# Reordering the end of a one-core attention and spectral-mixing kernel: two pairs' sums set into the last modes, their transposes set ahead of the seventh chunk

## The chip, the cores and the metric

One core of a Trainium2 chip. The metric is device microseconds of one execution, the median of several. "The clock" below is the granted clock of TensorE, 1.00 at full speed.

## The reference, cut to what matters

Causal attention gives x, of 8 batches x 576 positions x 512 channels. Then:

```
X = rfft(x, axis=1)[:, :64]                       # 64 modes
Y = X (complex) times w_r + i w_i, mode by mode   # 64 matrices of 512 x 512, twice
y = irfft(Y, n=576)
u = x + y
out = u + max(u @ w_ch, 0)
```

The kernel streams the 64 + 64 weight matrices from HBM all through the attention. `u @ w_ch` is computed as `x @ w_ch + G (Y @ w_ch)`, where G is the inverse transform as a matrix, so that only the part with Y has to wait for the weights.

## The kernel before: the parts that matter

The modes come in 8 chunks for each of 4 groups of input channels. `modes(g, c)` runs one chunk: sixteen matmuls of 32 columns out of four weight tiles (two of w_r, two of w_i, in the order in which they are loaded). In the last group each chunk is finished: `y_sb` (the sum, by VectorE), `yt` (transposed on TensorE, copied by ScalarE to `yt_sb`), `v` (y @ w_ch, four matmuls, cast by VectorE). Both the rows of y and those of v are spread by DMA into `yv`, from where the inverse transform reads them.

```python
def modes(g, c):
    ps = auxpool.tile([P, DM], FP32, name="yp", tag="aux")
    for x in range(4):                       # four weight tiles
        ...
        for cg in range(4):
            nc.tensor.matmul(ps[32 * cg : 32 * cg + 32, :], ..., wt[(g, c, ri, par)][:, cg, :],
                             start=(x == 0), stop=(x == 3), tile_position=(0, 32 * cg), ...)
    ...                                      # last group: y_sb = ps + y_acc, then
    spread(c, 0, yb)                         # DMA of the rows of y into yv

def x_transposed(i):                         # a pair = two blocks of 128 positions
    for x, (b, T) in enumerate(pairs[i]):
        ps = upool.tile([P, DT, P], FP32, name="xt_ps", tag="u")     # two buffers
        ...                                  # 4 transposing matmuls
        nc.vector.tensor_copy(out=xts[i][:, x], in_=ps)
```

The end of the kernel, after the sixth chunk (c = 5) is done:

```python
c = NCK - 2                                  # the seventh chunk
yb = modes(NG - 1, c)
x_transposed(0)
yt = y_transposed(yb)
x_transposed(1)
y_times_wch(c, yt)                           # v, and its spread into yv
for i in range(NPRE):                        # NPRE = 2 pairs
    x_times_wch(i, False)                    # z = x @ w_ch, 8 matmuls each

start_u(0)                                   # u = x of pair 0
add_y(us[0], 0, 0, slice(0, GK))             # u += G y, chunks 0 to 6
for i in range(NPRE):
    add_y(z_of(i), i, 1, slice(0, GK))       # z += G (y @ w_ch), chunks 0 to 6
yb = modes(NG - 1, NCK - 1)                  # the last modes
...                                          # yt, v, then the last chunk's share of u and z
```

The softmax here doesn't subtract the row's maximum and nothing guards it: scores larger than these inputs give would overflow.

## Time and profile before

| | |
|---|---|
| time, median of 6 (first 3 known at the prediction) | 462.47 us (462.04 to 462.76) |
| TensorE, VectorE, ScalarE, GpSimd busy | 74%, 51%, 48%, 40% |
| chain that ended last | DMA 66%, TensorE 20% |
| last wait for weights on that chain ends | 398.31 us of a span of 460.6 |

How to read it: no engine is full, and the DMA row of the page is full through slice 36 of 40. The kernel waits for weights until 398 us, and the last 62 us are a chain of TensorE work. The change lies between 411 and 423 us. The lines of that stretch are in the prediction.

### The profile page before, as it was taken

What the parts mean: (1) busy time and instruction counts of PE and PEld (TensorE: products, weight loads), DVE (VectorE), ACT (ScalarE), POOL (GpSimd) and SP (SyncE); (2) the same over time, 40 slices, a digit from 0 to 9 for tenths busy, and PEclk for the clock granted to TensorE, in tenths of its full rate; (3) what the DMA queues carried; (4) which work ended last, traced back from release to release, by engine and by line L of the source; (5) the groups of instructions that cost most, each with busy time, mean ns of one, the idle gap of its engine ahead of it and who ended that gap; (6) DMA issues with size and microseconds to landing.
All of it is one profiled execution on the core that took longest, in us unless ns stands there. A gap on an engine that the chain in (4) does not pass through costs nothing.

```text
span 460.6 us, 10231 instructions
## 1 busy us (share of the span) xinstructions
PE 342.9 (74%) x4153; PEld 216.4 (47%) x4185; DVE 233.5 (51%) x523; ACT 219.2 (48%) x382; POOL 182.8 (40%) x269
## 2 busy tenths in 40 slices
PE   1779877966663969947397676888977766589995
PEld 1456655644442646624265444565643432244442
DVE  6775665653332646623254435467544432162675
ACT  1585876554342737734255434466710202040895
POOL 6755545534445455344454443455232232100000
PEclk9997999997777979968778979799987789599999
DMA  9999999999999999999999999999999999993697
GB/s 175 201 203 203 202 201 203 203 204 204 204 204 200 203 199 203 204 205 204 202 200 205 204 204 204 204 202 203 206 210 214 214 214 214 214 210 81 228 309 297
DMA packets 110063, 95.16 MB, mean 207 GB/s; under 512 B 28544, under 2 KB 105216, under 8 KB 110016
## 3 DMA queue, kind: packets, MB, share of 16 engines
q0 software_dynamic: 98960, 81.81, 112.1%
q1 hardware_dynamic: 11056, 12.70, 8.9%
q8 instruction: 33, 0.54, 0.4%
q14 instruction: 14, 0.11, 0.1%
HBM read 164.66 MB, written 9.44 MB: 378 GB/s over the span
## 4 chain that ended last, share of the span: by engine, by line
DMA 66%; PE 20%; DVE 6%; issue 4%; POOL 2%; SPq 0%; DVEq 0%; POOLq 0%
DMA w_sb<-in_moe_w_i_dram 29%; DMA w_sb<-in_moe_w_r_dram 20%; DMA q<-in_q_dram 15%; PE z_ps L595 3%; PE sc_ps L365 2%; PE z_ps L654 2%; PE tr_ps L324 2%; PE yp L438 2%; PE u_ps L673 2%; PE u_ps L654 2%; PE sc_ps L359 2%; PE z_ps L774 1%; PE av_ps L394 1%; POOL w_sb L217 1%; DMA xs<-c_negm 1%
## 5 line engine op out<-in xcount | busy, mean ns | idle before, releaser
L373 ACT ACTIVATE p_sb<-sc_ps,cumt_sb 128x576 f16<-128x576 f32 (+1 forms) x256 | 142.0, 635 | 47.1 <-PE sc_ps L365 46.7
L217 POOL DMA_DIRECT2D w_sb<-in_moe_w_i_dram x60 | 45.0, 750 | 79.9 <-PE yp L438 33.5
L217 POOL DMA_DIRECT2D w_sb<-in_moe_w_r_dram x60 | 45.3, 756 | 69.0 <-DMA w_sb<-in_moe_w_r_dram 30.9
L217 POOL DMA_DIRECT2D v<-in_v_dram x72 | 50.7, 707 | 32.4 <-DMA w_sb<-in_moe_w_r_dram 7.8
L438 PE MATMUL yp<-w_sb,xs 128*32 128x512 bf16 x480 | 38.1, 414 | 26.1 <-DMA w_sb<-in_moe_w_i_dram 21.2
L359 PE MATMUL sc_ps<-negm,ident 128*128 128x256 bf16 x256 | 56.3, 306 | 0.2
L324 PE MATMUL tr_ps<-ident,q 64*64 64x64 bf16 x576 | 17.7, 212 | 51.7 <-DMA q<-in_q_dram 51.7
L327 DVE COPY qtA<-tr_ps 64x576 bf16<-64x576 bf16 x32 | 23.7, 742 | 47.4 <-PE tr_ps L324 47.4
L394 PE MATMUL av_ps<-v,p_sb 128*128 128x65 f16 x1024 | 45.0, 199 | 0.0
L344 ACT ACTIVATE p<-sc_ps,cumt 128x64 f16<-128x64 f32 x32 | 10.0, 313 | 73.2 <-PE sc_ps L340 73.2
L394 PEld LDWEIGHTS <-p_sb 128*128 128x128 f16 x1024 | 40.1, 101 | 5.1 <-issue 1.2
L327 DVE COPY ktA<-tr_ps 64x576 bf16<-64x576 bf16 x32 | 24.0, 749 | 32.8 <-PE tr_ps L324 32.8
L438 PEld LDWEIGHTS <-xs 128*32 128x32 bf16 x512 | 22.6, 170 | 37.5 <-issue 34.0
L324 PEld LDWEIGHTS <-q 64*64 64x64 bf16 x576 | 13.8, 124 | 54.4 <-DMA q<-in_q_dram 53.3
L365 PE MATMUL sc_ps<-qtB,ktB 128*128 128x64 bf16 (+2 forms) x160 | 35.2, 326 | 3.7 <-issue 2.4
L365 PE MATMUL sc_ps<-qtA,ktA 65*128 65x512 bf16 (+2 forms) x192 | 37.3, 304 | 0.3 <-DVE ktA L327 0.3
L399 DVE TENSOR_REDUCE den<-av_ps 128x5 f32<-128x10 f32 x64 | 10.8, 169 | 48.6 <-PE av_ps L394 48.6
L404 DVE TENSOR_TENSOR x_all<-av_ps,rcp 128x320 f16<-128x320 f32 x64 | 31.4, 491 | 2.2
L327 ACT COPY ktB<-tr_ps 64x576 bf16<-64x576 bf16 x32 | 20.3, 634 | 20.3 <-DVE ktA L327 19.2
L365 PEld LDWEIGHTS <-ktB 128*128 128x128 bf16 x192 | 22.7, 118 | 15.2 <-issue 6.6
L595 PE MATMUL z_ps<-wch_sb,xs 128*128 128x512 f16 x96 | 28.4, 452 | 0.0
L324 PE MATMUL tr_ps<-ident,k 64*64 64x64 bf16 x576 | 17.4, 209 | 14.5 <-DVE qtB L327 10.7
(103 smaller groups left out, 517.2 us busy)
## 6 DMA issues: line engine op xcount, KB each, us to landing
w_sb<-in_moe_w_r_dram POOLq DMA_DIRECT2D x60, 512.0 KB, 11.9
w_sb<-in_moe_w_i_dram POOLq DMA_DIRECT2D x60, 512.0 KB, 11.9
q<-in_q_dram POOLq DMA_DIRECT2D x32, 144.0 KB, 9.7
k<-in_k_dram POOLq DMA_DIRECT2D x32, 144.0 KB, 10.0
v<-in_v_dram POOLq DMA_DIRECT2D x72, 64.0 KB, 9.8
out_dram<-r_sb SPq DMA_DIRECT2D x16, 256.0 KB, 2.4
out_dram<-r_w SPq DMA_DIRECT2D x16, 256.0 KB, 2.5
x_all<-in_moe_w_i_dram POOLq DMA_DIRECT2D x3, 512.0 KB, 9.8
```

Of the source, the lines that this page charges most:

```text
L217: nc.gpsimd.dma_start(out=dst, in_=src)
L324: nc.tensor.transpose(ps[rows, r, :], src[rows, r, :], ident16[rows, rows])
L327: copy(out=dst[n % NQ][rows, :].rearrange("d (p r) -> d p r", r=R), in_=ps[rows].rearrange("d r p -> d p r"),)
L359: nc.tensor.matmul(ps[:, bass.ds(w * S, W)], ident16, negm[:, bass.ts(r, W)], start=True, stop=False, skip_group_check=True,)
L365: nc.tensor.matmul(ps[:, c0 : c0 + i1 - i0], keys[:, w, r, :], qt[:, i0:i1], start=False, stop=True, skip_group_check=True,)
L373: nc.scalar.activation(out=pt[:, poff[x] : poff[x] + S - w * W], in_=ps[:, w * S : (w + 1) * S - w * W], func=ACTF.Exp, bias=cumt_sb[:, x, ...
L394: nc.tensor.matmul(ps[:, I, r : r + NCH], lhsT, rhs, start=(i == 0), stop=(i == len(todo) - 1), skip_group_check=True,)
L399: nc.vector.tensor_reduce(out=den, in_=ps[:, :, 0 : VW : NCH], axis=mybir.AxisListType.X, op=ALU.add)
L404: nc.vector.tensor_tensor(out=x_all[:, g, b, :, D * h : D * h + D], in0=ps[:, :, 1 : NCH], in1=rcp.unsqueeze(2).to_broadcast([P, NT, D]), ...
L438: nc.tensor.matmul(ps[32 * cg : 32 * cg + 32, :], cols[:, c0 : c0 + 32, c * MC + 2 * cg + par], wt[(g, c, ri, par)][:, cg, :], start=(x == ...
L595: nc.tensor.matmul(z[:, x, :], xts[i][:, x, dt, :], wch_sb[:, dt, :], start=(dt == 0), stop=(last and dt == DT - 1), skip_group_check=True,)
L654: nc.tensor.matmul(dst[x][r, :], G_sb[rows, bass.ds(T * P, r.stop - r.start)], yv[rows, bb, which, :], start=start, stop=True, skip_group_ ...
```

## The change

Intent: give TensorE something to do while it waits for the last weight tile of the last modes (the z sums of two pairs), and while it waits for the seventh chunk's tiles (the transposes of x of these pairs). No instruction is added or removed.

```diff
-    def modes(g, c):
+    def modes(g, c, meanwhile=None):
...
+            if x == 3 and meanwhile:
+                meanwhile()
             for cg in range(4):
...
     c = NCK - 2
+    for i in range(NPRE):
+        x_transposed(i)
     yb = modes(NG - 1, c)
-    x_transposed(0)
     yt = y_transposed(yb)
-    x_transposed(1)
     y_times_wch(c, yt)
...
-    for i in range(NPRE):
-        add_y(z_of(i), i, 1, slice(0, GK))
-    yb = modes(NG - 1, NCK - 1)
+    def first_sums():
+        for i in range(NPRE):
+            add_y(z_of(i), i, 1, slice(0, GK))
+    yb = modes(NG - 1, NCK - 1, first_sums)
```

## The prediction

> **What bounds the kernel now.** I read the page first. Its engine rows show no engine above 74% busy, but its DMA row stands at 9 or more through slice 36 of 40: for most of the span the weight stream is the bound, and the chain that ended last is 66% DMA. The change touches only the last 10%, so I cut the chain of waits to that part.
>
> ```profile
> 398.31 0.04 issue
> 398.36 0.67 PE yp L438 x3
> ...
> 411.47 1.08 PE yp L438 x15
> 412.55 0.02 issue
> 412.57 0.04 DVE y_sb L452
> ...
> 413.18 1.29 DVE xs L589 x2
> 414.47 0.04 issue
> 414.51 0.38 PE xt_ps L585 x4
> 414.89 0.86 PE v_ps L621 x4
> 415.75 3.45 PE z_ps L595 x16
> 419.21 0.43 PE u_ps L673 x2
> 419.64 0.54 PE u_ps L654 x2
> 420.18 0.34 issue
> 420.52 1.02 PE z_ps L654 x4
> 421.54 1.09 PE yp L438 x12
> 422.63 0.02 issue
> 422.65 0.44 DVE y_sb L452
> ```
>
> The columns are start, duration and what held the chain. The last weight wait on the chain ends at 398.31 us. From there to 455 us it is a chain of TensorE work and of copies TensorE waits for. The seventh chunk's modes (411.47) and the last modes (421.54) both start because TensorE got to them, not because a tile arrived. The DMA view gives the w_i tiles a landing of about 21 us after issue. The last one was issued at 398.85 us, so it was there at about 420.2 us, 1.3 us before the last modes began. The seventh chunk's last tile, issued at 387.4 us, was there at about 408.9 us, 2.5 us before its modes. **So the wait that this change is built to fill is hardly there.**
>
> The TensorE timeline of the stretch has all the waits there are:
>
> ```profile
> 412.45 0.62 PE L585 MATMUL xt_ps<-ident16h,x_all 128*128 128x128 f16 x8
> 413.32 0.40 PE L613 MATMUL yt_ps<-ident16h,y_sb 128*128 128x128 f16 x4 [0.25 <-DVE y_sb L452]
> 413.91 0.38 PE L585 MATMUL xt_ps<-ident16h,x_all 128*128 128x128 f16 x4 [0.20 <-DVE xs L589]
> 414.51 0.38 PE L585 MATMUL xt_ps<-ident16h,x_all 128*128 128x128 f16 x4 [0.21 <-DVE xs L589]
> ```
>
> Idle time stands in the brackets: 0.25, 0.20 and 0.21 us, then the 0.34 us ahead of the z sums, which is the arrival of the seventh chunk's y@w_ch rows (issued at 416.51 us, 3.9 us to landing, so 420.4 us). In all 1.0 us in eleven. The transposes of x are what fills the waits of the chain y_sb, yt, yt_sb, v here.
>
> **What the Trainium skill says.** "TensorE: Matmul & The Clock Gate", Part 3, The mechanism: matmuls start and end in program order, only weight loads are pulled ahead. The trace agrees as far as it goes: the z sums wait 0.34 us and the last modes, whose data are there, stay behind them. The same page, Back-to-back issue gap, gives 518 cycles for 512 columns at 2.4 GHz; here 16 matmuls take 3.45 us, 0.216 us each. The same page, Part 1, What's actually happening: half clock after an idle window of about 3.4 us on a free-running grid. The trace agrees on the grid and says how idle: reading windows of 3.41 us aligned on the clock drop at 389.25 us, 1.65 us of TensorE work (338.05 us) was followed by half clock and 1.96 us (382.42 us) was not. "DMA: Bandwidth & Descriptors", Issuing engines are not separate DMA queues: transfers from all issuing engines share the 16 DMA engines and interleave. The trace agrees: a 128 KB spread into yv takes 6.2 us beside the weight stream and 2.9 us after it.
>
> **The change part by part.** No instruction is added or removed; the order listing shows 32 transposing matmuls (counting their loads) moved and 4 z-sum matmuls moved on TensorE, and the seventh y_sb add placed behind the four casts of transposed x on VectorE. I walk the stretch with the durations above, from 411.40 us, where TensorE is free of the last kept product in both kernels.
>
> Transposes ahead of the seventh modes. The first eight take 8 x 0.055 = 0.44 us, from 411.40. VectorE is on the cast of the sixth chunk's v rows until 411.78, so its casts of 0.62 us start at about 411.82. The u buffers are two: the third group of transposes needs the first cast, the fourth the second. In the kernel before, those groups started 0.73 and 1.33 us after the first cast began; so they start at 412.55 and 413.15 here. The first wait (from 412.0, with the drain) is about 0.55 us, the second 0.22. The seventh modes then start at 413.37 instead of 411.40: +1.97 us, of which 0.88 is the transposes themselves.
>
> The seventh chunk's chain without filling. Modes to y_sb: 1.17 us (411.40 to 412.57 before), so y_sb at 414.54; the casts are done by 414.3, so VectorE is free. From y_sb to the first v matmul an unfilled chain took 1.88 us in the chunk at 387.41 to 389.29 us (add 0.69, transposes 0.40, copy 0.58 and three hand-overs). So v at 416.42 us instead of 414.73: **+1.69 us**. TensorE idles some 0.75 us ahead of yt and 0.7 us ahead of v, which the transposes filled before. TensorE's idle time up to v is about 2.2 us against 0.66 us; the 1.5 us agrees with the +1.69, the rest being drains counted as busy.
>
> The products after it do not wait: v 0.86, z 3.45, u 0.43 and 0.43 us, so u is done at 421.6 against 419.9 by the same sum.
>
> The sums between the third and the last weight tile. Twelve mode matmuls at 0.065 us take 0.79 us, to 422.4. The v rows are issued at about 418.2 (v start + 1.8 us, as before); with a landing of 2.9 to 3.9 us that is 421.1 to 422.1, just ahead. So the 0.34 us wait and its 0.1 us of restart are gone, and the last tile, there since about 420.2, is not waited for in either order. Sums 0.9 us, last four modes and drain 0.38 us: the last y_sb at about 423.7 us against 422.65.
>
> Sum: +1.69 from the transposes, -0.6 from the sums' new place (the wait removed, hand-overs), **+1.1 us**. From y_sb on the chain is unchanged and TensorE is 100% busy to 450 us, so nothing absorbs it: 462.7 + 1.1 = **463.8 us**.
>
> **The rivals.**
> 1. The clock drops. In the window 413.14 to 416.55 us my walk leaves TensorE about 0.4 (last transposes) + 1.0 to 1.2 (modes) + 0.4 (yt) + 0.1 (v) = 1.9 us busy, against 2.82 before. That is on the edge between 1.65 (dropped) and 1.96 (did not). A drop at 416.55 would run the v and z matmuls at half rate for one window, 3.41 us, costing about 1.7 us: 465.5. For it: the margin is nothing, and the grid may lie otherwise in other executions. Against: the smallest sliding window I find holds 1.8 us[...]. I give it one in six.
> 2. The change wins. If the last tile came later than I read, or the seventh chunk's, the transposes would cost nothing and the sums would fill a real wait. For it: the DMA row still carries traffic to 419.5 us, so the last tile is the last thing to arrive. Against: both modes started with no weight wait, with 1.3 and 2.5 us in hand. The sums' part alone is worth at most some 0.5 us: 462.2. One in eight for a time under the one of before.
> 3. It is hidden. Later seventh rows find an emptier DMA, so the yv landings move less than the issues, and the walk's idle times shrink if VectorE starts its casts earlier. That gives 463.0. The end has no slack of its own, so full hiding is unlikely.
>
> **Range and chances.** Centre 463.8; below it rival 3 and part of 2, above it the clock. Range 462.4 to 465.9 us. Two per cent is 9.3 us, which no rival reaches: even a clock drop with a late landing stays under 467. Within 2%: 0.98; 0.01 on each side.
>
> **What would show it.** Right: in the changed kernel the seventh modes start near 413.4 us with waits on the casts ahead of them; yt and v of that chunk wait 0.7 us each on y_sb and the copy; the first three weight tiles' twelve matmuls stand ahead of the z sums with no wait; the last y_sb add starts near 423.7 us; from there on both traces are the same. Wrong: a weight-tile wait in either place, a granted clock of 0.5 after 416 us, or a z sum that waits for the v rows. What would make it wrong: a weight stream that ends later in this execution, or transposes that find VectorE free.

## The result and the profile after

463.69 us (463.29 to 464.18, 6 runs) against 462.47 us. A ratio here is the mean time of one kernel's runs over that of the other's of the same rounds, so not quite the ratio of the medians; it is 1.0028, with a 95% interval of 1.0015 to 1.0041. Executions over 1.5% slower than the fastest of the same kernel are left out of the means. The kernel got slower by 1.2 to 1.3 us; at the 2% line it is the same.

The chain of waits of the changed kernel, in the stretch that the prediction shows of the kernel before (start us, duration us, what held the chain):

```profile
413.21 0.38 PE xt_ps L588 x4
413.59 1.08 PE yp L441 x13
...
414.70 0.70 DVE y_sb L455
...
415.45 0.41 PE yt_ps L616 x4
...
415.94 0.59 ACT yt_sb L618
...
416.58 1.04 PE v_ps L624 x4
417.61 3.45 PE z_ps L598 x16
421.07 0.43 PE u_ps L676 x2
421.50 0.51 PE u_ps L657 x2
422.01 0.84 PE yp L441 x10
422.85 0.97 PE z_ps L657 x4
423.81 0.43 PE yp L441 x4
...
424.26 0.44 DVE y_sb L455
```

The y_sb add, the yt transposes, the yt_sb copy and v follow each other here one by one. Before, the first three did not stand on the chain (y_sb for 0.04 us only), because transposes of x ran beside them. The z sums now stand inside the last modes without any wait, where before there was an "issue" of 0.34 us ahead of them. The last y_sb add starts at 424.26 us against 422.65.

TensorE's own timeline has its waits in brackets (idle time, and what ended it):

```profile
412.61 0.38 PE L588 MATMUL xt_ps<-ident16h,x_all 128*128 128x128 f16 x4 [0.56 <-DVE xs L592]
413.21 0.38 PE L588 MATMUL xt_ps<-ident16h,x_all 128*128 128x128 f16 x4 [0.21 <-DVE xs L592]
415.45 0.40 PE L616 MATMUL yt_ps<-ident16h,y_sb 128*128 128x128 f16 x4 [0.80 <-DVE y_sb L455]
416.58 1.04 PE L624 MATMUL v_ps<-wch_sb,yt_sb 128*128 128x512 f16 x4 [0.73 <-ACT yt_sb L618]
421.40 0.61 PE L657 MATMUL u_ps<-yv,G_sb 112*128 112x512 f16 x2
```

These are 2.30 us of idle up to v, against 0.66 us before. The last line has no bracket, but it stands 0.07 us later than two matmuls of 0.216 us behind the start of u would put it: the seventh chunk's rows of y, issued at 415.42 us and 5.9 us on their way, landed at 421.3 us. The kernel before was already as close (0.09 us late by the same sum, its rows issued at 413.29 us and 6.2 us on their way). That will matter.

The clock stayed up. The view by windows, in the windows of 3.41 us aligned on this trace's rise of the clock at 402.22 us (window, its length, busy time of each engine with its instructions, granted clock, DMA share, GB/s):

```profile
412.46:415.87 3.41, 2.22 (x28) 1.33 (x27) 2.58 (x5) 0.20 (x1) 0.00 (x0) 1.00 1.18 204
415.87:419.29 3.42, 2.71 (x13) 1.29 (x14) 0.69 (x1) 0.58 (x1) 0.00 (x0) 1.00 0.58 122
```

The emptiest window kept 2.22 us of TensorE work and the next ran at clock 1.00, so nothing of the loss is clock. The grid lay kindly in this trace: windows set 0.6 to 1 us later would hold 1.83 to 1.88 us. But two runs below with the same emptied waits met such a window, 1.89 us from 412.72 us in the transposes alone and 1.88 us from 415.12 us in the unfilled run with late rows, and there too the next window ran at clock 1.00.

The whole span can't be compared from one trace to the other: the changed kernel's trace had its last weight wait end 0.93 us later, and got 0.8 us of that back because its clock rose earlier. So I measure from S, the start of the eight matmuls of the last kept product (x @ w_ch of a later pair, computed ahead and kept; 409.58 us before, 409.72 after), ahead of everything the change touches:

| trace | S to the seventh chunk's v | S to the last y_sb add | S to the end |
|---|---|---|---|
| before | 5.15 | 13.07 | 51.02 |
| changed | 6.86 | 14.54 | 52.48 |

The loss is 1.71 us at v, 1.47 us at the last y_sb add, and 1.46 us at the end of the span: it is made in this stretch. Behind it two small differences cancel. The last chunk's v rows took 3.1 us to land against 2.9 and stand on the chain of the changed kernel, so that the last r_sb add (VectorE's last work) starts 48.02 us after S against 46.37, 1.65 us later. From there to the end, while the last outputs land, it is 4.46 us against 4.65. This last piece runs from 4.37 to 4.91 us over all twelve traces, with no pattern by variant, so an end of a span is good to some 0.5 us only.

### The profile page after: what moved, and what is told of

Read it like the earlier page. It is cut to its first block, busy times and chain, and to the rows that moved or that the text cites. A ratio compares the mean times of both kernels' runs of the same rounds, so it can differ in the third digit from the quotient of the medians.

```text
span 462.2 us, 10263 instructions
## 1 busy us (share of the span) xinstructions
PE 345.9 (75%) x4185; PEld 215.8 (47%) x4185; DVE 233.6 (51%) x523; ACT 219.1 (47%) x382; POOL 182.9 (40%) x269
## 4 chain that ended last, share of the span: by engine, by line
DMA 66%; PE 22%; issue 4%; DVE 4%; POOL 3%; ACT 0%; DVEq 0%; POOLq 0%; ACTq 0%
DMA w_sb<-in_moe_w_i_dram 40%; DMA w_sb<-in_moe_w_r_dram 8%; DMA q<-in_q_dram 7%; DMA k<-in_k_dram 5%; PE yp L441 3%; PE av_ps L394 2%; PE sc_ps L365 2%; DMA x_all<-in_moe_w_r_dram 2%; PE z_ps L598 2%; DMA y_acc<-in_moe_w_r_dram 2%; PE z_ps L657 2%; DMA y_acc<-in_moe_w_i_dram 2%; PE u_ps L676 2%; PE tr_ps L324 2%; PE u_ps L657 2%
## 5 line engine op out<-in xcount | busy, mean ns | idle before, releaser
L365 PE MATMUL sc_ps<-qtB,ktB 128*128 128x512 bf16 (+2 forms) x192 | 42.3, 336 | 0.0
L327 ACT COPY ktB<-tr_ps 64x576 bf16<-64x576 bf16 x32 | 20.3, 633 | 21.4 <-DVE ktA L327 20.4
## 6 DMA issues: line engine op xcount, KB each, us to landing
w_sb<-in_moe_w_r_dram POOLq DMA_DIRECT2D x60, 512.0 KB, 11.9
w_sb<-in_moe_w_i_dram POOLq DMA_DIRECT2D x60, 512.0 KB, 11.9
```

Source lines behind the costliest of these rows:

```text
L327: copy(out=dst[n % NQ][rows, :].rearrange("d (p r) -> d p r", r=R), in_=ps[rows].rearrange("d r p -> d p r"),)
L365: nc.tensor.matmul(ps[:, c0 : c0 + i1 - i0], keys[:, w, r, :], qt[:, i0:i1], start=False, stop=True, skip_group_check=True,)
```

## The experiments

Ten kernels, all correct, in three batches, each on one chip with its own runs of the kernel before (medians 462.59, 462.82 and 462.40 us, 11 runs each). The batches were: the two parts, one pair and the fourth kernel below called "sums behind the modes"; then the filled waits, two breaks and two more attempts; then the two with late rows. Theory A was that of the prediction: the transposes used to fill waits, and their move empties them. The rivals: B, breaking the last modes in two costs; C, chance in the weight stream and clock.

### The two parts alone

First the sums alone (`meanwhile` as in the change, transposes as before):

```diff
-    for i in range(NPRE):
-        add_y(z_of(i), i, 1, slice(0, GK))
-    yb = modes(NG - 1, NCK - 1)
+    yb = modes(NG - 1, NCK - 1, first_sums)
```

> The kernel before with one part of the change alone: the y@w_ch sums of the first two pairs stand between the third and the last weight tile, the transposes of x stay where they were. Theory A (the loss comes from the transposes, which filled the waits of the seventh chunk's chain; the sums' place is a small gain): the 0.34 us wait ahead of the z sums goes, so 0.2 to 0.5 us under the kernel before, about 462.2 us, and the last y_sb add starts near 422.3 us against 422.65. Theory B (breaking the last modes in two is what costs): about 1.2 us over the kernel before, 463.7 us, as the whole change. Theory C (the difference is in how the weight stream and the clock fell, not in the order): within 0.2 us of the kernel before.

Measured 461.93 us, ratio 0.9994 (0.9980 to 1.0008). The stretch in the trace is clearer: 12.74 us to the last y_sb add, 0.33 us less than before, and TensorE's timeline shows the sums reached without a wait:

```profile
419.88 0.90 PE L440 MATMUL yp<-w_sb,xs 128*32 128x512 bf16 x12
420.71 1.04 PE L656 MATMUL z_ps<-yv,G_sb 112*128 112x512 f16 x4
421.68 0.47 PE L440 MATMUL yp<-w_sb,xs 128*32 128x512 bf16 x4
```

So this part is a gain of a third of a microsecond in the trace, too small for the timed interval. B falls as the cause of the loss; what a break itself costs is measured below.

Then the transposes alone (sums as before):

```diff
+    for i in range(NPRE):
+        x_transposed(i)
     yb = modes(NG - 1, c)
-    x_transposed(0)
     yt = y_transposed(yb)
-    x_transposed(1)
```

> The kernel before with the other part alone: both pairs' transposes ahead of the seventh chunk, the sums ahead of all of the last modes as before. Theory A: the seventh chunk's v matmuls start about 1.8 us later than before; the sums don't wait, as the v rows have landed by then; so 1.3 to 1.7 us over the kernel before, about 464.0 us, at or a little above the whole change. Theory B: the kernel before's time. Theory C: within 0.2 us of the kernel before.

Measured 463.25 us, ratio 1.0017 (1.0003 to 1.0030): 0.8 us of loss by the ratio, less than expected. S to v is 6.85 us, as in the whole change, so the +1.7 us at v is the transposes' alone, and C falls. But the last y_sb add comes at 14.18 us, 0.36 us earlier than in the whole change, with no wait ahead of the sums:

```profile
421.15 1.02 PE L654 MATMUL z_ps<-yv,G_sb 112*128 112x512 f16 x4
422.10 1.12 PE L438 MATMUL yp<-w_sb,xs 128*32 128x512 bf16 x16
```

With the transposes moved, the v rows have landed by the time TensorE comes to the sums; moving the sums as well has no wait left to fill. From the first of these matmuls to the y_sb add it takes 2.13 us unbroken and 2.32 us broken, in the changed kernel as in the first run. The difference is still there at the last r_sb add (47.64 us after S against 48.02); that the ends of the two spans differ by 0.02 us is the landing of the last outputs, 4.86 us against 4.46. So in the trace the sums' place costs 0.4 us next to moved transposes; the timed intervals overlap, so in time it is not shown.

### One pair's transposes only

```diff
+    x_transposed(0)
     yb = modes(NG - 1, c)
-    x_transposed(0)
     yt = y_transposed(yb)
     x_transposed(1)
```

> Half of the second part: only the first pair's transposes go ahead of the seventh chunk, the second pair's stay between yt and v; the sums as before. Theory A says that the cost is emptied waits and not the moved work: the first eight transposes find both u buffers free and wait for no cast, and the second eight still fill the wait for the yt copy, so v starts at most 0.3 us later than before and the time is within 0.3 us of the kernel before, not half-way to the second run. A rival that charges by the amount of work moved ahead gives half of it, 0.7 to 0.9 us over.

Measured 462.99 us, ratio 1.0012 (0.9998 to 1.0025), some 0.5 us over, so the expected time was missed by its middle value, more than half-way to the second run's 0.8 us after all (the interval alone would still admit the 0.3 us). The part about TensorE held: S to v is 5.32 us, 0.17 more than before, and no transpose waits for a cast. The loss came later, where I had not looked: y_sb of the seventh chunk was 0.45 us later, its rows were issued and landed later, so that u's sums of y stand 0.29 us later than the two matmuls ahead of them allow (issue at 413.65, 6.2 us to landing, start at 419.85), and the z sums waited 0.65 us (0.34 before). To the last y_sb add it is 13.74 us, +0.67. So there is a second path beside TensorE's: y_sb, the spread, and some six microseconds of landing.

### The waits filled again

The whole change, but with seven of the sixteen x @ w_ch products of these pairs in the two emptied waits:

```diff
     for i in range(NPRE):
         x_transposed(i)
     yb = modes(NG - 1, c)
+    some_products(4)
     yt = y_transposed(yb)
+    some_products(3)
     y_times_wch(c, yt)
-    for i in range(NPRE):
-        x_times_wch(i, False)
+    some_products(len(pending))              # the other nine
```

> The whole change, with the two waits that it empties filled again by other work: four of the sixteen x@w_ch products of these pairs stand between the seventh modes and yt, three between yt and v, the rest behind v as before. Theory A (the loss is TensorE idle in those two waits, 0.80 and 0.73 us in the changed kernel): v starts within 0.2 us of the changed kernel's, and the products behind it end 1.3 to 1.5 us earlier. What then comes of it depends on the rows of y, which are issued no earlier and land about 5.9 us after issue, at 421.3 us on the changed kernel's clock: u, which would be reached at 420.0, waits for them for over 1 us, so that only 0.2 to 0.5 us of 1.4 reach the end, about 463.3 us. If those rows land as the queue empties, sooner, up to 1.2 us reach the end, 462.5 us.

Measured 463.87 us (462.77 to 466.33), ratio 1.0020 (0.9997 to 1.0044): no gain over the changed kernel that the times can show, though the filling itself worked. The wait for the rows had been written down beforehand; that nothing of the gain would reach the end had not. TensorE reached u 9.68 us after S, 1.50 us earlier than in the changed kernel, and then stood still. TensorE's timeline, then the chain of waits:

```profile
419.69 0.59 PE L675 MATMUL u_ps<-x_all,ident16h 128*128 128x512 f16 x2
421.71 0.60 PE L656 MATMUL u_ps<-yv,G_sb 112*128 112x512 f16 x2 [1.43 <-DMA yv<-y_sb]
```

```profile
415.71 5.96 DMA yv<-y_sb
...
421.71 0.60 PE u_ps L656 x2
```

The last y_sb add is at 14.56 us, against 14.54 unfilled. Theory A as I had it is not enough. The changed kernel has two paths of almost the same length from the late seventh modes to u: TensorE's with its emptied waits, and the rows of y with their landing. Shortening one alone shows nothing. That is theory D.

### Two by two: waits empty or filled, rows needed early or late

To take the rows off the path I let nothing that reads them stand ahead of the last modes. Both runs keep all transposes ahead of the seventh chunk:

```diff
     start_u(0)
-    add_y(us[0], 0, 0, slice(0, GK))
-    yb = modes(NG - 1, NCK - 1, first_sums)
+    yb = modes(NG - 1, NCK - 1)
+    add_y(z_of(0), 0, 1, slice(0, GK))
 ...
+    add_y(us[0], 0, 0, slice(0, GK))
     add_last(us[0], 0, yb)
 ...                                          # v of the last chunk
+    add_y(z_of(1), 1, 1, slice(0, GK))
```

> Both pairs' transposes ahead as in the changed kernel, waits left empty, but no sum that needs the seventh chunk's rows of y or y@w_ch stands ahead of the last modes: the first z sums stand behind the modes, u's sums ahead of its last ones, the second z sums behind the last v matmuls. With the run whose waits are filled and the next one this makes a table of two by two: waits empty or filled, rows needed early or late. Theory D (two paths of the same length set the changed kernel's stretch, TensorE's emptied waits and the landing of the rows of y some 6 us after a later issue; so either alone doesn't help): with the rows out of the way the emptied waits remain, v starts 6.85 us after the last kept product, the last y_sb add at about 12.8 us after it (14.54 in the changed kernel, 13.07 before), and 0.4 us of moved sums come back behind it: about 0.2 us over the kernel before. Theory A alone (only the emptied waits): the same, so it is the next run that tells.

> The same with both waits filled by products, seven of sixteen. Theory D: filling, which was worth nothing while the rows were needed early (14.56 against 14.54 us to the last y_sb add), is worth 1.0 to 1.5 us now, unless the last tile is waited for: the last y_sb add at 11.4 to 11.9 us, and a time 0.7 to 1.2 us under the kernel before, though all transposes stand ahead of the seventh chunk. If filling is worth under 0.4 us here too, the loss is not in those waits and theory D falls.

Unfilled: 462.84 us, ratio 1.0006 (0.9993 to 1.0019). Filled, with the same `some_products` as above: 461.09 us, ratio 0.9977 (0.9962 to 0.9993). In the traces, S to the last y_sb add, and S to the last r_sb add (the fairer one here, since the late rows also put work behind the y_sb add, and it leaves out the landing of the last outputs):

| | waits empty | waits filled | filling is worth |
|---|---|---|---|
| rows needed early (changed kernel, waits filled) | 14.54 / 48.02 | 14.56 / 48.03 | -0.02 / -0.01 |
| rows needed late | 12.89 / 46.63 | 11.38 / 45.26 | 1.51 / 1.37 |

TensorE's timeline of the filled run: the last modes start straight behind u, and the 0.46 us of idle ahead of the z sums lie beside the y_sb add, which starts at 420.45 us (the v rows, issued at 417.73 us and 3.0 us on their way, had only just landed):

```profile
419.27 1.12 PE L438 MATMUL yp<-w_sb,xs 128*32 128x512 bf16 x16
420.85 0.59 PE L654 MATMUL z_ps<-yv,G_sb 112*128 112x512 f16 x2 [0.46 <-issue]
```

Both came as written down, but for 0.02 us of the second run's y_sb add (11.38 us, where 11.4 to 11.9 was said). Filling is worth nothing while the rows are on the path, and 1.4 to 1.5 us once they are off it. Theory D stands. What the table does not separate: the late rows also leave the modes unbroken and put sums into the wait for the last y_sb add, so the gain from row one to row two is not the landing alone.

### What a break in the modes costs

The changed kernel with two breaks of two matmuls in place of one of four:

```diff
-    yb = modes(NG - 1, NCK - 1, first_sums)
+    yb = modes(NG - 1, NCK - 1, {
+        2: lambda: add_y(z_of(0), 0, 1, slice(0, GK)),
+        3: lambda: add_y(z_of(1), 1, 1, slice(0, GK)),
+    })
```

> What breaking the last modes costs by itself: the changed kernel with the first pair's sums between the second and third tile and the second pair's between the third and last, so two breaks of two matmuls each in place of one of four; all the work is the same. From the first of these matmuls to the last y_sb add the traces of unbroken modes show 2.13 us and of one break 2.32 us. If each change between full-width and 32-column matmuls costs about 0.1 us, this run shows 2.45 to 2.6 us and a time 0.1 to 0.3 us over the changed kernel, 463.9 us. If the 0.19 us had been a wait for the last tile or the rows, it shows 2.3 us.

Measured 464.52 us (463.37 to 466.30), ratio 1.0033 (1.0016 to 1.0050), not apart from the changed kernel's 1.0028. In the trace it is 2.62 us from the first line below to the last y_sb add at 425.10, against 2.32 with one break and 2.13 with none:

```profile
422.48 0.69 PE L440 MATMUL yp<-w_sb,xs 128*32 128x512 bf16 x8
423.10 0.61 PE L656 MATMUL z_ps<-yv,G_sb 112*128 112x512 f16 x2
423.64 0.47 PE L440 MATMUL yp<-w_sb,xs 128*32 128x512 bf16 x4
424.04 0.60 PE L656 MATMUL z_ps<-yv,G_sb 112*128 112x512 f16 x2
424.57 0.47 PE L440 MATMUL yp<-w_sb,xs 128*32 128x512 bf16 x4
```

Two z matmuls take 0.54 us from their start to that of the modes behind them (423.10 to 423.64), where two in a row need 0.43. A break costs 0.2 to 0.3 us of TensorE, with all data there. The Trainium skill, "TensorEngine Tiling (Array Packing)", Key Properties, says that a change of tiling mode drains TensorE; these 0.1 us at each change agree with it, but no run here shows the drain itself.

### Attempts to beat both kernels

Sums behind the modes: transposes as in the kernel before; the first pair's sums behind all of the last modes, where TensorE waits for y_sb, the second's behind the last v:

```diff
-    for i in range(NPRE):
-        add_y(z_of(i), i, 1, slice(0, GK))
     yb = modes(NG - 1, NCK - 1)
+    add_y(z_of(0), 0, 1, slice(0, GK))
 ...                                          # yt, v
+    add_y(z_of(1), 1, 1, slice(0, GK))
```

> An attempt to beat both: transposes as in the kernel before, but the first pair's sums behind all of the last modes, where TensorE waits 0.54 us for the y_sb add, and the second pair's behind the last v matmuls. If TensorE's waits are what counts from here on: the 0.34 us wait and most of the 0.54 us wait go, so 0.6 to 1.1 us under the kernel before, about 461.7 us. If another engine sets the end from here on, no gain; if the last tile lands later than the modes now start (420.0 us), part of the gain is a weight wait.

Measured 461.10 us, ratio 0.9972 (0.9958 to 0.9985), 1.3 us under the kernel before, a little more than expected. To the last y_sb add it is 11.82 us, and from there to the end 37.96 us, as before (37.95): the sums behind it cost nothing, as they lie in its waits.

```profile
419.55 1.34 PE L438 MATMUL yp<-w_sb,xs 128*32 128x512 bf16 x16
...
420.94 0.76 DVE L452 TENSOR_TENSOR y_sb<-yp,y_acc 128x256 f16<-128x256 f32 x2 [4.91 <-PE yp L438]
```

The modes took 1.34 us instead of 1.12: the last tile, issued at 399.02 us with 21.4 us to landing, came at 420.4, and they waited 0.2 us for it. Only now is that tile on the path.

Then more of the same:

```diff
+    x_transposed(0)
     yb = modes(NG - 1, c)
-    x_transposed(0)
-    yt = y_transposed(yb)
     x_transposed(1)
+    yt = y_transposed(yb)
+    some_products(4)
     y_times_wch(c, yt)
 ...
+    yb = modes(NG - 1, NCK - 1, <u's sums of pair 0>)   # z sums as in the run above
```

> An attempt to beat the fourth run: the first pair's transposes ahead of the seventh modes (no cast wait), the second pair's behind them, four products between yt and v, and u's sums of y between the third and last tile, the z sums placed as in the fourth run. Up to the last products TensorE should gain 0.5 to 0.7 us on the fourth run. In the fourth run the last modes already stood 0.2 us for the last tile; if the arrival of that tile is now the bound, the gain isn't seen at the last y_sb add: time within 0.4 us of the fourth run (about 461.0 us), with the wait ahead of the last four modes grown to 0.5 us or more. If TensorE's own work is still the bound, 460.5 us.

Measured 461.42 us, ratio 0.9966 (0.9954 to 0.9978), not apart from the run above in time, as was expected, though the last y_sb add comes at 11.46 us against 11.82. The bound named beforehand was wrong. It was not the tile but the rows of y (issued at 414.25, 6.2 us to landing) that held TensorE:

```profile
420.49 0.60 PE L656 MATMUL u_ps<-yv,G_sb 112*128 112x512 f16 x2 [0.18 <-DMA yv<-y_sb]
```

The last variant set the first pair's z sums ahead of the last tile too (`rows_before` = u's sums and z sums of pair 0):

> As the sixth kind of order (first pair's transposes ahead, products in the wait), but with the first pair's z sums also ahead of the last tile, and the second pair's in the wait for the y_sb add. If the last tile's arrival is the bound, work put ahead of it is free and this gains 0.2 to 0.4 us on the run before the last: about 460.7 us. If the v rows land after the tile (issued at about 416.7 us, 3.9 to 4.5 us to landing, so 420.6 to 421.2), the z sums hold the last tile's modes up and it loses 0.3 to 0.7 us instead.

Measured 462.03 us, ratio 0.9987 (0.9972 to 1.0002): a loss against the run before of 0.6 us by the medians, which is the size written down, and of 1.0 us by the ratios, whose intervals just meet. It came through another row than expected (the profiled execution, 463.44 us, was one of two that took 1.3 us or more longer than the other four): in its trace the rows of y took 7.0 us to land and u waited 0.97 us for them, inside the modes, with the last tile's four matmuls behind them. So here work that depends on a late transfer must not stand ahead of work that the end depends on.

## Why the prediction was right

- **The time.** 463.8 us was said, 463.69 us came. In time the loss was 1.2 to 1.3 us, 1.1 was said. That the total came within 0.1 us is in part luck: it stood on 462.7 us, the median of three runs, where six give 462.47, and this made up for a loss put too low.
- **No weight wait to fill.** Right: in neither kernel do the last or the seventh modes wait for a tile. Only the faster variants come near the last tile.
- **The transposes, +1.69 us at v.** Right: 1.71 us, in the change and in the run with the transposes alone (1.70). The waits were 0.56 and 0.21 us on the casts (0.55 and 0.22 said) and 0.80 and 0.73 us ahead of yt and v (0.75 and 0.7 said). What failed is what the prediction took this for. It is not enough to have the waits filled: the filled run shows that the later y_sb alone, by way of its rows' landing, gives the same loss. The prediction looked at the landing of the v rows and not at that of the y rows, which came at 421.3 us, when TensorE was there too.
- **The sums, -0.6 us.** The term that was mis-sized. From v to the last y_sb add the change gained 0.24 us. The run with the transposes alone gained 0.59 without moving the sums at all, as the v rows have landed by then; the new place then takes 0.36 us of it back, 0.19 in the break and the rest in a later start of the modes and of u. The prediction counted the wait's end to the sums' credit and gave the break no cost. It said 423.7 us for the last y_sb add, 423.84 on the other trace's S; it was 424.26.
- **The clock rival, one in six.** It didn't come about: 2.22 us of TensorE work in the emptiest window, where 1.9 was estimated, and clock 1.00 behind it. The estimate was for another place of the grid and good for that (1.88 us from 413.28 us in this trace); two other runs had 1.88 and 1.89 us in a window of their own grid and kept the clock. So the margin that the prediction could not settle, between 1.65 and 1.96 us, was on the safe side, which its figures did not show.
- **The rival that the change wins.** Wrong for the change, right for the sums alone: 0.33 us in the trace, where at most some 0.5 was said.
- **The rival that it is hidden.** The landings did shorten, as it said (the rows of y 5.9 us against 6.2, those of v 3.3 against 3.9), but the casts' waits did not shrink, and nothing was hidden.
- **No slack at the end.** Right in the main: from the last y_sb add to the end it is 37.95 us before and 37.94 us after, though the start of the last r_sb add is 0.18 us further behind it (33.48 us against 33.30). But TensorE is not 100% busy from there to 450 us, as was said: it waits 0.54 us for the y_sb add at once, the wait that the sums behind the modes fill.

## What to carry to other kernels

Before filling a wait, look whether it is there: here the tile it was for had landed some 1.3 us before the last modes began, while the moved work was filling real waits elsewhere. When a stage comes later, follow every product of it to its reader, the transfers as well as the next engine: two paths of the same length hide each other, and shortening one shows nothing until the other is out of the way. In this kernel filler did best behind the work that the end depends on, and did harm where it read what landed late.

## What the Trainium skill lacked or had wrong

- "TensorE: Matmul & The Clock Gate", Part 1: it gives the grid of about 3.4 us and the half clock after an idle window, not how little work counts as idle. Here 1.65 us of TensorE work in an aligned window of 3.41 us was followed by half clock (and 1.68 us from 371.50 us in the changed kernel's trace), and 1.88, 1.89, 1.96 and 2.22 us were not.
- "TensorEngine Tiling (Array Packing)", Key Properties: a change of mode drains TensorE, without a figure. Here one break of 32-column matmuls by full-width ones took 0.19 us (2.13 to 2.32 us) and a second 0.30 us more (2.62 us).
- "DMA: Bandwidth & Descriptors", Issuing engines are not separate DMA queues: it says that transfers interleave, without a figure for what that does to a small one. Here the same 128 KB spread took 4.5 to 7.4 us when it was issued beside the weight stream (up to 416.1 us of the span) and 2.9 to 4.9 us when it was issued behind it.
